# Eight-batch cached attention and dense layers, decode step: a scaled mask for one half of the last batch, and a re-listed order of tasks

## The chip, the cores and the metric

The kernel runs on one core of one Trainium2 chip. The metric is the device time of one execution in microseconds (us). A core has TensorE (PE, with its weight loads shown apart as PEld), VectorE (DVE), ScalarE (ACT), GpSimd (POOL) and SyncE (SP), which here only issues the transfers. The engines run at the same time and wait for each other through semaphores. Lines such as L878 are lines of the kernel before.

## The reference

Eight batches with one query token each (width 448) go through two equal layers. Layer 2 is the same mathematics with the same weights and the same caches.

```python
W = min(4096, max(256, Sk // 4))                       # 1024 keys
q = (x @ wq).reshape(B, Sq, 16, 256)
k, v = the last W rows of k_cache, v_cache, each of 8 heads repeated twice
scores = einsum("bhqd,bhkd->bhqk", q, k) * (256 ** -0.5)
o = einsum("bhqk,bhkd->bhqd", softmax(scores), v) ... @ wo
x = x + A(layernorm(x));  x = x + silu(layernorm(x) @ w1) @ w2     # twice
```

The layer norm divides by the deviation of x. In layer 2 the kernel leaves this division to the end: the query is built from x and its mean only, the scores of all keys are taken with it, and the softmax multiplies them by 1/deviation on the way into the exponential.

## The kernel before, in words

Keys and values of a batch (8 heads, each 512 KB of keys and as much of values) are loaded once and used by both layers. They go through a ring of 30 slots of one head each; every slot is loaded in two halves of 256 KB. SP issues the loads in a fixed order, keys of a batch and then its values. A load waits until its slot has been given back, and until the load ten halves ahead of it has landed. A key slot is given back when layer 2's scores of its four heads are done, a value slot when layer 2's products with the values are. The weights (wq first, wo, w1 and w2 after the first batch) are loaded once.

For each batch, in this order of dependence:

- **KT** (L1238): VectorE turns the 16 key halves in place, 32 x 32 blocks, one instruction each.
- **S0**, layer 1 scores (L878), for all 8 heads; maximum (max0, L889), two small turns and a minimum that bring the maxima of a row together (L896, L898, L901), exponential (L908), transposition of the probabilities on TensorE (pT, L914) and copy (L923), row sums (l, L927) and reciprocal (L932).
- **PV0** (L947), products with the values, in steps for heads 0 to 3 and 4 to 6, and head 7 in another form (L981); `oev` (L952) copies them out, `oT` (L954) transposes; **wor** (L998) multiplies by wo; `fold` (L1014, L1015) brings rows back to columns.
- **chain**: statistics (s12, L1032; m2, mean, va; a reciprocal root by two Newton steps on VectorE), **w1** (L839), its turn (L848), the activation, **w2r** (L998 again), fold, statistics of layer 2 (Newton steps on POOL, L746 to L762, whose result is 1/deviation).
- Layer 2's query, once for heads 0 to 3 and once for 4 to 7: **wq** (L1100, 16 matmuls), turn **qT** (L1105), selection **qsel** (L1111), **qf** (L1117, adds the mean's part, which ScalarE has written at L1091) and **qbd** (L1118), which spreads the query over the four blocks of 32 partitions by multiplying it with a mask of ones and zeros.
- **S1**, layer 2 scores (L878 again), separately for the two halves, the same softmax with 1/deviation as the exponential's scale, and PV1 (L947). Only in the last batch is the softmax itself done for each half apart, as soon as its scores are there. In layer 2 the negated maximum, which is the exponential's bias, is first multiplied by 1/deviation too: **mbs1** (L905).

After batch 7, `final` does layer 2's output product and dense part for all batches at once (L1127 to L1212).

The batches overlap: batch b's layer 2 runs among the steps of batch b+1's layer 1. Each engine executes its instructions in one list, fixed when the program is built. A planner (`schedule`, twice, with priorities from a backward pass `tails`) lists the tasks by estimated costs. It also puts in **fillers** on TensorE (L1282), matmuls that compute nothing and add zero, at places where the planner sees TensorE waiting. Then `best_schedule` goes through the table `MOVES`: an entry `i:j` takes task i out of its engine's list and puts it back directly ahead of task j, one after the other. The task numbers count the tasks in the order in which they are added; the fillers come last, from 1672 on. Those that matter below:

| number | task |
|---|---|
| 217, 245 | s12 of batch 0, first and second |
| 226 to 230, 237 | w1 and w2r of batch 0 |
| 261 to 264, 266 | wq and qsel of batch 0, heads 0 to 3 |
| 265, 267, 268 | qT, qf, qbd of batch 0, heads 0 to 3 |
| 277 to 280 | S1 of batch 0, heads 0 to 3 |
| 346 to 361 | the 16 key turns of batch 1 |
| 362 to 365 | S0 of batch 1 |
| 885 to 888, 869 | PV1 of batch 3, heads 4 to 7, and its row sums |
| 1697, 1704, 1706 to 1715 | fillers |

In the list of before TensorE runs, in batch 0: fold 239, s12 245, wq 261 to 264, x_init of batch 1, fillers 1706, 1708 and 1704, qsel 266. VectorE runs: turns 346 to 349, qT 265, qf 267, turn 352, qbd 268, and then the eleven other turns of batch 1. `rstds[1]` is 1/deviation of layer 2.

Of the kernel before, what the change touches and what calls it, by code (L numbers as in the profile page):

```python
# [51 lines left out]

MOVES = {
# [8 lines left out]
    "dve":  # L62
# [5 lines left out]
    "act":  # L68
# [3 lines left out]
    "pool":  # L72
        "",
}
# [385 lines left out]
def bass_interleave_layers__sliding_block_cached__dense_activation_silu__decode_kernel(  # L460
# [121 lines left out]
    def bk(i):  # L582
        return [("bank", i)]
# [306 lines left out]
            mseg[layer][:, ks[0]:ks[-1] + 1], bank[sc][:, lo:hi].rearrange("p (k n) -> p k n", k=len(ks)), AX.X, ALU.max,  # L890
            negate=True), bk(sc), [("mseg", layer, k) for k in ks], 0.42 if len(ks) == 1 else 0.7, "max%d" % layer)

    def softmax(b, layer, ks, sc):
        lb, ei, mT = LB[layer], layer, mTs[layer]
        row_max(layer, ks, sc)
        dve(lambda e: e.transpose(mT, mseg[ei]), [k for k in MROW[ei] if k[0] != "mT"], [("mT", ei)],  # L896
            0.21, "mT%d" % layer)
        dve(lambda e: e.tensor_reduce(  # L898
            mg[ei][:, 0:4].rearrange("p (k r) -> p k r", r=2),
            mT[:, 0:16].rearrange("p (k q r) -> p k r q", k=2, r=2), AX.X, ALU.min), [("mT", ei)], [("mg", ei)], 0.16, "mg%d" % layer)  # L900
        dve(lambda e: e.transpose(mb[ei].rearrange("p (k q r) -> p k q r", k=4, r=2),  # L901
                                  mg[ei][:].rearrange("p (k r) -> p k r", r=2).unsqueeze(2).broadcast_to([P, 4, 4, 2])),
            [("mg", ei)], [k for k in MROW[ei] if k[0] != "mT"], 0.21, "mb%d" % layer)
        if layer:
            act(lambda e: e.activation(mb[ei][:, 0:2], mb[ei][:, 0:2], ACTF.Copy, scale=rstds[1][:, 0:1]),  # L905
                MSEG[ei] + [("rstd", 1)], MSEG[ei], 0.2, "mbs1")
        for k2 in ks:
            act(lambda e, k2=k2: e.activation(  # L908
                e_sb[ei][:, k2, :, :].rearrange("p uh (jj ul) -> p uh jj ul", ul=2),
                bank[sc][:, k2 * 256:(k2 + 1) * 256].rearrange("p (ul uh jj) -> p uh jj ul", ul=2, uh=4),  # L910
                ACTF.Exp, bias=mb[ei][:, k2:k2 + 1],
                scale=rstds[1][:, 0:1] if layer else 1.0), bk(sc) + [MSEG[ei][k2]] + ([("rstd", 1)] if layer else []), [("e", ei, k2)] + ([] if layer or not k2 else ["rowpad"]), 0.56 if layer else 0.475, "exp%d" % layer)
        for k2 in ks:
            pe([lambda e, uh=uh, ql=ql, k2=k2: e.matmul(  # L914
                bank[lb][64 * ql:64 * ql + 64, k2 * 64:k2 * 64 + 64].rearrange(
                    "p (j q u r) -> p u j q r", j=4, q=2, u=4)[:, uh],
                e_sb[ei][:, k2, uh, :],
                ident[:].rearrange("p (j x) -> p j x", j=4)[:, :, 8 * k2:8 * k2 + 8].rearrange(
                    "p j (qh ql r) -> p j qh ql r", qh=2, ql=2)[:, :, :, ql, :],
                start=True, stop=True, tile_position=(0, 64 * ql)) for uh in range(4) for ql in range(2)],  # L920
               [("e", ei, k2), "ident"] + ([] if layer or not k2 else ["rowpad"]), bk(lb), (16, 2), "pT%d" % layer)
        k0, k1 = ks[0], ks[-1] + 1
        act(lambda e: e.activation(  # L923
            pT_sb[ei][:, k0:k1].rearrange("p k n u r -> p (k n u r)"), bank[lb][:, k0 * 64:k1 * 64], ACTF.Copy),
            bk(lb), [("pT", ei, k) for k in ks], 0.28, "pTev%d" % layer)
        nk = k1 - k0
        pe([lambda e, u=u, qh=qh: e.matmul(  # L927
            bank[lb][:, C_L:C_L + 8 * nk], ones_b,
            pT_sb[ei][:, k0:k1].rearrange("p k (j q) u r -> p k j q u r", q=2)[:, :, :, qh, u, :],
            start=(u == 0 and qh == 0), stop=(u == 3 and qh == 1)) for u in range(4) for qh in range(2)],  # L930
           [("pT", ei, k) for k in ks] + ["ones_b"], bk(lb), (8 * nk, 1), "l%d" % layer)
        dve(lambda e: e.reciprocal(rl_sb[ei][:, 8 * k0:8 * k1], bank[lb][:, C_L:C_L + 8 * nk]), bk(lb),  # L932
            [("rl", ei, k) for k in ks], 0.25, "rl%d" % layer)
# [138 lines left out]
    def chain(b):  # L1072
# [20 lines left out]
        for k2 in range(2):  # L1093
            parts = [(XB, 0, DH), (YB, DH, DH)] if (tail or WQS) and k2 == 0 else [(XB, 0, 2 * DH)]
            for wb, h0, n in parts:
                for c in range(KC):
                    fns = []
                    for j in range(4):
                        off = (c * HD if c < 3 else 3 * HD - k2 * 2048) + (4 * k2 + j) * 512 + h0
                        fns.append(lambda e, j=j, c=c, wb=wb, off=off, h0=h0, n=n, k2=k2: e.matmul(  # L1100
                            bank[wb][32 * j:32 * j + 4, h0:h0 + n], xn[:, part(c, k2), j, :],
                            wq_sb[:, off:off + n], start=(c == 0), stop=(c == KC - 1),
                            tile_position=(0, 32 * j), skip_group_check=True))
                    pe(fns, [("xn", max(0, part(c, k2) - 2))] + WQ_R, bk(wb), (n, 4), "wq")
                dve(lambda e, wb=wb, h0=h0, n=n: e.transpose(  # L1105
                    qT[:, h0:h0 + n].rearrange("p (c a i) -> p c a i", a=2, i=32),
                    bank[wb][:, h0:h0 + n].rearrange("p (c i a) -> p c a i", a=2, i=32)),
                    bk(wb), (QT0 if h0 == 0 else []) + (QT1 if h0 + n > DH else []), 0.18 + n / 950.0, "qT")
            lb = LB[1]
            qs = bank[lb][:, C_Q + 64 * k2:C_Q + 64 * k2 + 64]  # L1110
            pe([lambda e, qs=qs, j=j: e.matmul(  # L1111
                qs[32 * j:32 * j + 32].rearrange("p (k c r) -> p k r c", k=4, c=8), irep,
                qT[:].rearrange("p (r c i) -> p i r c", r=2, i=32)[:, 0:4],
                start=True, stop=True, tile_position=(0, 32 * j)) for j in range(4)], QT0 + QT1 + ["irep"], bk(lb),
               (256, 4), "qsel")
            qf, QF = mrow[1 - k2][:], MROW[1 - k2]
            dve(lambda e, qs=qs, qf=qf: e.tensor_tensor(qf, qs, qf, ALU.add), bk(lb) + QF, QF, 0.25, "qf")  # L1117
            (pool if k2 and not tail else dve)(lambda e, k2=k2, qf=qf: e.tensor_tensor(  # L1118
                qbd[1][:, :, k2, :].rearrange("p n (q r) -> p n q r", r=2),
                qf.rearrange("p (n r) -> p n r", r=2).unsqueeze(2).broadcast_to([P, 32, 4, 2]),  # L1120
                mask.unsqueeze(1).unsqueeze(3).broadcast_to([P, 32, 4, 2]), ALU.mult),
                QF + MASK_R, [("qbd", 1, k2)], 0.55 if k2 and not tail else 0.4, "qbd")

    def rows8(banks, n, w_sb, rhs, reads, name):
        for i0 in range(0, n, 4):
# [132 lines left out]
    def layer2(b):  # L1258
        chain(b)
        last = b == NB - 1  # L1260
        for k2 in range(2):
# [2 lines left out]
            freed.update((b, "k", 4 * k2 + j) for j in range(4))  # L1264
            pump()
            if last:
                softmax(b, 1, (k2,), sc)
        if not last:
            softmax(b, 1, (0, 1), SC[1])
        for k2 in range(2):  # L1270
# [50 lines left out]
```

## Time and profile before

| | |
|---|---|
| median of 3 runs | 242.47 us (242.2 to 242.66) |
| the profiled execution | 243.63 us, its span 241.9 us |
| busy: PE, DVE, ACT, POOL | 188.5, 152.6, 86.7, 26.2 us |
| read from memory | 77.67 MB, mean 321 GB/s over the span |
| shares of the chain that ended last | PE 46%, DMA 18%, DVE 18%, ACT 7%, SP's queue 5% |

The span counts from the first to the last instruction; the device time of the same execution is 1.73 us longer. "Busy" counts an engine's instructions, whether or not anything waits for them. The chain follows the work back from the last instruction: at each step to what released it, or to the instruction before it on its engine. The transfers fill the first 200 us; the last key and value loads are issued at 193.3 and 203.5 us, and from 212 us on nothing but the computation of the last batch is left.

### The profile page before, as it was taken

To read this page: it belongs to the slowest core of one execution; us is meant where nothing else is said; L and a number is where in the kernel's file an instruction comes from. 1 tells how busy PE (TensorE), PEld (TensorE's weight loads), DVE (VectorE), ACT (ScalarE), POOL (GpSimd) and SP (SyncE) were. 2 spreads that over 40 slices of the span, in tenths; PEclk is the share of its full clock that TensorE was granted. 3 is DMA by queue.
4 is the path that set the end of the run, shared out by engine and by line. 5 is a ranking of instruction groups with operands and counts; after the bars stand their busy time and mean duration, and the time that the engine had idled before them with its cause. 6 is when DMAs were issued, how large, how long until landed. Compare 5 with 4: busy or idle time off the path is not lost.

```text
span 241.9 us, 8437 instructions
## 1 busy us (share of the span) xinstructions
PE 188.5 (78%) x3537; PEld 97.5 (40%) x3567; DVE 152.6 (63%) x425; ACT 86.7 (36%) x292; POOL 26.2 (11%) x125
## 2 busy tenths in 40 slices
PE   1052648878969888978897988889878999899884
PEld 1051113322335345534452544355344535446552
DVE  7359420045964995796489559956985896334433
ACT  2004041023034524541644163446426440543431
POOL 6100000002010031003000300210031004003000
PEclk9999999997999999999999999999999999999999
DMA  5999999999999999999999999999999989300000
GB/s 221 377 365 403 407 400 382 391 377 406 402 406 401 342 384 375 395 340 390 323 387 395 387 348 397 378 379 380 395 397 391 385 278 403 139 3 4 3 3 1
DMA packets 40341, 78.22 MB, mean 323 GB/s; under 512 B 4320, under 2 KB 6512, under 8 KB 39792
## 3 DMA queue, kind: packets, MB, share of 16 engines
q1 hardware_dynamic: 40304, 77.69, 86.9%
q8 instruction: 28, 0.46, 0.7%
q14 instruction: 9, 0.07, 0.1%
HBM read 77.67 MB, written 0.01 MB: 321 GB/s over the span
## 4 chain that ended last, share of the span: by engine, by line
PE 46%; DMA 18%; DVE 18%; ACT 7%; SPq 5%; issue 4%; POOL 1%; DVEq 0%; ACTq 0%
DMA ring<-in_A_k_cache_dram 10%; PE bank L947 10%; DVE ring L1238 8%; PE bank L878 7%; DMA w2o<-in_B_w_dram 6%; PE bank L998 6%; PE bank L1100 4%; PE bank L1282 3%; PE bank L1111 3%; ACT qT L908 3%; SPq L679 3%; DMA ring<-in_A_v_cache_dram 3%; DVE mrow L889 2%; PE bank L914 2%; PE bank L954 2%
## 5 line engine op out<-in xcount | busy, mean ns | idle before, releaser
L1238 DVE STREAM_TRANSPOSE ring<-ring 128x512 uint32<-128x512 uint32 x128 | 81.2, 683 | 9.5 <-DMA ring<-in_A_k_cache_dram 9.5
L878 PE MATMUL bank<-ring,qbd 128*16 128x512 bf16 (+2 forms) x768 | 35.9, 324 | 5.1 <-DVE ring L1238 4.1
L947 PE MATMUL bank<-ring,pT_sb 128*4 128x512 bf16 (+1 forms) x512 | 36.5, 378 | 0.1
L1282 PE MATMUL bank<-wq_sb,smalls 128*128 128x512 bf16 x99 | 29.2, 400 | 0.9 <-issue 0.7
L878 PEld LDWEIGHTS bank<-ring,qbd 128*16 128x16 bf16 (+1 forms) x768 | 19.3, 91 | 18.7 <-DVE ring L1238 5.0
L855 ACT ACTIVATE qbd<-q1s 32x128 bf16<-32x128 bf16 x32 | 10.3, 321 | 46.0 <-PE bank L878 45.4
L1100 PE MATMUL bank<-wq_sb,xn 128*4 128x512 bf16 (+1 forms) x272 | 18.3, 384 | 0.6 <-ACT xn L1082 0.3
L889 DVE TENSOR_REDUCE mrow<-bank 128x2 f32<-128x512 f32 (+1 forms) x17 | 10.9, 643 | 11.8 <-PE bank L878 10.1
L1014 ACT ACTIVATE qT<-bank 128x448 bf16<-128x448 f32 x16 | 8.7, 544 | 24.7 <-PE bank L998 24.7
L914 PE MATMUL bank<-ident,qT 128*64 128x16 bf16 x256 | 8.4, 182 | 10.9 <-ACT qT L908 10.5
L1282 PEld LDWEIGHTS bank<-wq_sb,smalls 128*128 128x128 bf16 x129 | 10.8, 100 | 12.5 <-issue 8.2
L947 PEld LDWEIGHTS bank<-ring,pT_sb 128*4 128x4 bf16 (+1 forms) x512 | 11.2, 84 | 10.5 <-issue 1.6
L998 PE MATMUL bank<-w2o,oT 128*1 128x448 bf16 x224 | 13.2, 352 | 0.2 <-DMA w2o<-in_A_wo_dram 0.2
L1105 DVE STREAM_TRANSPOSE qT<-bank 128x512 f32<-128x512 f32 (+1 forms) x17 | 11.3, 665 | 2.7 <-PE bank L1100 2.7
L952 ACT ACTIVATE qT<-bank 128x512 bf16<-128x512 f32 x16 | 9.6, 597 | 9.3 <-PE bank L947 5.9
L914 PEld LDWEIGHTS bank<-ident,qT 128*64 128x64 bf16 x256 | 6.2, 113 | 13.9 <-ACT qT L908 13.0
L952 ACT ACTIVATE qbd<-bank 128x512 bf16<-128x512 f32 (+1 forms) x16 | 9.1, 570 | 4.9 <-PE bank L947 3.0
L746 POOL TENSOR_SCALAR smalls<-smalls 128x1 int32<-128x1 int32 x8 | 1.5, 191 | 85.2 <-ACT smalls L1047 55.9
L1111 PE MATMUL bank<-qT,w2o 128*32 128x64 f32 x128 | 8.4, 353 | 2.4 <-DVE qT L1105 1.6
L1249 POOL MEMSET qT<- 128x64 bf16 x8 | 1.2, 153 | 82.5 <-PE bank L954 75.6
L908 ACT ACTIVATE qT<-bank,mrow 128x256 bf16<-128x256 f32 x16 | 6.8, 471 | 7.6 <-DVE mrow L901 7.4
L1042 DVE SCALAR_TENSOR_TENSOR smalls<-bank,smalls 128x1 f32<-128x1 f32 x8 | 1.2, 149 | 12.9 <-ACT smalls L1040 9.4
(182 smaller groups left out, 255.3 us busy)
## 6 DMA issues: line engine op xcount, KB each, us to landing
ring<-in_A_k_cache_dram SPq DMA_DIRECT2D x128, 256.0 KB, 5.9
ring<-in_A_v_cache_dram SPq DMA_DIRECT2D x128, 256.0 KB, 6.3
w2o<-in_A_wo_dram SPq DMA_DIRECT2D x2, 1792.0 KB, 13.0
wq_sb<-in_A_wq_dram SPq DMA_DIRECT2D x3, 1024.0 KB, 6.9
w2o<-in_B_w_dram SPq DMA_DIRECT2D x1, 1568.0 KB, 14.2
w_sb<-in_B_w_dram SPq DMA_DIRECT2D x3, 448.0 KB, 11.6
wq_sb<-in_A_wq_dram SPq DMA_DIRECT2D x2, 256.0 KB, 10.3
w_sb<-in_B_w_dram SPq DMA_DIRECT2D x2, 112.0 KB, 11.4
```

Of the source, the lines that this page charges most:

```text
L878: fns.append(lambda e, cb=cb, par=par, j=j, kv=kv, m=m, c0=c0, c1=c1: e.matmul(bank[sc][32 * j:32 * j + m, c0:c1], qbd[layer][:, j * 8 + c ...
L889: dve(lambda e: e.tensor_reduce(mseg[layer][:, ks[0]:ks[-1] + 1], bank[sc][:, lo:hi].rearrange("p (k n) -> p k n", k=len(ks)), AX.X, ALU.m ...
L908: act(lambda e, k2=k2: e.activation(e_sb[ei][:, k2, :, :].rearrange("p uh (jj ul) -> p uh jj ul", ul=2), bank[sc][:, k2 * 256:(k2 + 1) * 2 ...
L914: pe([lambda e, uh=uh, ql=ql, k2=k2: e.matmul(bank[lb][64 * ql:64 * ql + 64, k2 * 64:k2 * 64 + 64].rearrange("p (j q u r) -> p u j q r", j ...
L947: fns.append(lambda e, qh=qh, uh=uh, j=j, vv=vv: e.matmul(bank[ob][32 * j:32 * j + 2 * w, 0:w * DH], p_col(ei, k2, j, qh, uh, w), vv, star ...
L952: act(lambda e: e.activation(o_sb[oi][:, 0:w * DH], bank[ob][:, 0:w * DH], ACTF.Copy), bk(ob), O_K[oi], 0.2 + w * 0.2, "oevh" if ob == OB[ ...
L998: pe([lambda e, i=i, c=c: e.matmul(bank[XB][32 * c:32 * c + 1, 0:D], rhs(i), w_sb[:, i * D:(i + 1) * D], start=(first and i - i0 < 4), sto ...
L1100: fns.append(lambda e, j=j, c=c, wb=wb, off=off, h0=h0, n=n, k2=k2: e.matmul(bank[wb][32 * j:32 * j + 4, h0:h0 + n], xn[:, part(c, k2), j, :],
L1105: dve(lambda e, wb=wb, h0=h0, n=n: e.transpose(qT[:, h0:h0 + n].rearrange("p (c a i) -> p c a i", a=2, i=32), bank[wb][:, h0:h0 + n].rearr ...
L1111: pe([lambda e, qs=qs, j=j: e.matmul(qs[32 * j:32 * j + 32].rearrange("p (k c r) -> p k r c", k=4, c=8), irep, qT[:].rearrange("p (r c i) ...
L1238: dve(lambda e, v=v: e.transpose(v, v), [("slot", s, h)], [("slot", s, h)], 0.67, "KT")
L1282: fills = {n: [lambda e, j=j, m=P // n: e.matmul(bank[OB[0]][m * j:m * j + m, 0:2 * DH], zero_b.broadcast_to([P, m]), wq_sb[:, 0:2 * DH], ...
```

## The change

In the last batch, for heads 4 to 7 only, ScalarE multiplies the mask by 1/deviation into four new columns (`masks`), and qbd uses this copy. So the scores of these heads come out scaled. Their softmax is called with `scaled=True`: mbs1 is left out, and the exponential's scale is the constant 1.0. One task is added and one goes away, so the tasks between them have numbers one higher than in before.

```diff
-    def softmax(b, layer, ks, sc):
+    def softmax(b, layer, ks, sc, scaled=False):
         lb, ei, mT = LB[layer], layer, mTs[layer]
+        scale, rk = (rstds[1][:, 0:1], [("rstd", 1)]) if layer and not scaled else (1.0, [])
...
-        if layer:
+        if rk:
             act(lambda e: e.activation(mb[ei][:, 0:2], mb[ei][:, 0:2], ACTF.Copy, scale=rstds[1][:, 0:1]),
...
-                scale=rstds[1][:, 0:1] if layer else 1.0), bk(sc) + ...
+                scale=scale), bk(sc) + ...
...
+            mkey, mk = MASK_R, mask
+            if tail and k2:
+                mkey, mk = ["masks"], smalls[:, 19:23]
+                act(lambda e: e.activation(smalls[:, 19:23], mask, ACTF.Copy, scale=rstds[1]), MASK_R + [("rstd", 1)], ["masks"], 0.2, "masks")
+            mk = mk.unsqueeze(1).unsqueeze(3).broadcast_to([P, 32, 4, 2])
...
-                softmax(b, 1, (k2,), sc)
+                softmax(b, 1, (k2,), sc, k2 == 1)
```

The table `MOVES` is replaced. The planner lists the changed tasks anew, and the table works on that list; 196 tasks stand elsewhere in the order than before. The entries that the prediction speaks of (those that are only in one of the two tables, except 1705:269, 277:272, 1709:1710 and 1714:280, which are in both):

```diff
 "pe"
-"1606:1573 1605:1559 888:869 887:888 1710:279 1704:266 1707:239 1697:1702"
+"1606:1574 1605:1560 888:876 1766:869 887:1766 1715:279 1710:1715 1706:1709 1697:245 1707:1697 1704:237"
 "pe", in both
 "1714:280 1709:1710 277:272 1705:269"
 "dve"
-"361:357 359:358 351:359 352:268"
+"351:360 354:353 350:267"
 "act"
-"1188:1176 1174:1173 1170:1174 1087:928 903:902 618:614 445:434 444:428 371:370 531:530 345:195"
+"1627:1626 1430:1235 1433:1432 1171:1188 1172:1171 1170:1173 1149:1147 986:985 963:961 1088:1087 1089:1088"
...
```

Task 876 is batch 3's first transposition after PV1, 1766 a filler. No entry of the new table names `masks` (1558).

More of the change, by code (lines that the diff above doesn't have):

```diff
@@ L911, in softmax @@
                 ACTF.Exp, bias=mb[ei][:, k2:k2 + 1],
-                scale=rstds[1][:, 0:1] if layer else 1.0), bk(sc) + [MSEG[ei][k2]] + ([("rstd", 1)] if layer else []), [("e", ei, k2)] + ([] if layer or not k2 else ["rowpad"]), 0.56 if layer else 0.475, "exp%d" % layer)
+                scale=scale), bk(sc) + [MSEG[ei][k2]] + rk, [("e", ei, k2)] + ([] if layer or not k2 else ["rowpad"]), 0.56 if layer else 0.475, "exp%d" % layer)
         for k2 in ks:
@@ L1117, in chain @@
             dve(lambda e, qs=qs, qf=qf: e.tensor_tensor(qf, qs, qf, ALU.add), bk(lb) + QF, QF, 0.25, "qf")
[L1118 to L1122, printed above, removed]
+            dst = qbd[1][:, :, k2, :].rearrange("p n (q r) -> p n q r", r=2)
+            qb = qf.rearrange("p (n r) -> p n r", r=2).unsqueeze(2).broadcast_to([P, 32, 4, 2])
+            mkey, mk = MASK_R, mask
[3 more added lines that the diff above has]
+            mk = mk.unsqueeze(1).unsqueeze(3).broadcast_to([P, 32, 4, 2])
+            (pool if k2 and not tail else dve)(lambda e, dst=dst, qb=qb, mk=mk: e.tensor_tensor(dst, qb, mk, ALU.mult),
+                                               QF + mkey, [("qbd", 1, k2)], 0.55 if k2 and not tail else 0.4, "qbd")
     def rows8(banks, n, w_sb, rhs, reads, name):
```

33 rows, old and new, of the table MOVES are left out of this document.

## Prediction, made before the result was known

> **What bounds the kernel now.** The profile of before spans 241.9 us, and the profiled execution took 243.63 us, 1.16 us above the median of the three runs, 242.47. I make the sum as differences inside that execution and take them off the median.
>
> I read the chain of waits first (start, length, what; the piece released the next one), in the stretch where batch 0 hands over to batch 1.
>
> ```profile
> 39.26 14.24 DMA w2o<-in_B_w_dram
> ...
> 56.17 1.81 PE bank L1100 x13
> ...
> 58.14 1.28 PE bank L1282 x3
> 59.42 0.49 PE bank L1111 x8
> ...
> 59.93 0.22 DVE mrow L1117
> 60.16 0.62 DVE ring L1238
> 60.78 0.31 DVE qbd L1118
> 61.08 6.57 DVE ring L1238 x11
> ...
> 67.69 1.04 PE bank L878 x16
> ...
> 147.04 5.26 DMA ring<-in_A_k_cache_dram
> ...
> 228.15 0.54 PE bank L947 x16
> ```
>
> Up to 53.5 us the second weight matrix is landing, so whatever the diff reorders before that is worth nothing. Then comes a piece in which no transfer is late: the 16 query matmuls (L1100), three fillers (L1282), the selection qsel (L1111), and on VectorE qf (L1117), one key turn (L1238), qbd (L1118) and eleven more turns. Only after the last turn can batch 1's scores (L878) start. So three fillers, which compute nothing, are on the path. (The last two lines are used further down.) The table by stretches (length, busy time and count of each engine, clock, DMA share, GB/s) shows why they are so long:
>
> ```profile
> 53.00:56.00 3.00, 1.30 (x23) 0.70 (x24) 1.87 (x3) 1.05 (x6) 0.00 (x0) 0.99 1.05 406
> 56.00:58.00 2.00, 2.00 (x23) 0.56 (x22) 0.71 (x2) 1.08 (x6) 0.83 (x5) 0.50 1.06 407
> 58.00:60.00 2.00, 2.00 (x13) 0.49 (x13) 0.78 (x2) 0.00 (x0) 0.94 (x5) 0.66 1.06 408
> ```
>
> TensorE's granted clock is 0.50 from about 56 us and 0.66 on average in the next 2 us: half clock for 2.0 + 2 x 0.34/0.5 = 3.4 us, right behind a stretch in which TensorE was busy for 1.30 of 3.00 us.
>
> VectorE's timeline there (the bracket is the idle time before, and who ended it):
>
> ```profile
> 54.13 2.58 DVE L1238 STREAM_TRANSPOSE ring<-ring 128x512 uint32<-128x512 uint32 x4 [1.63 <-DMA ring<-in_A_k_cache_dram]
> 58.02 0.72 DVE L1105 STREAM_TRANSPOSE qT<-bank 128x512 f32<-128x512 f32 x1 [1.32 <-PE bank L1100]
> 59.93 0.22 DVE L1117 TENSOR_TENSOR mrow<-bank,mrow 128x64 f32<-128x64 f32 x1 [1.19 <-PE bank L1111]
> ```
>
> VectorE stands still for 1.19 us ahead of qf, because qf is next in its order and qsel is late, while twelve turns wait behind it. From 61 us on those turns are the path.
>
> Whether time won at 67 us reaches the end depends on the loads. Two views speak to that: SP's waits (total, times, longest) and two stretches of the long table.
>
> ```profile
> SPq L710 <- PE bank L947: 15.1, 7, 3.0
> ```
> ```profile
> 50.00:75.00 25.00, 20.41 (x261) 8.14 (x264) 16.42 (x38) 6.57 (x25) 2.39 (x10) 0.93 1.05 402
> 100.00:125.00 25.00, 22.20 (x447) 11.43 (x452) 19.22 (x51) 11.18 (x37) 2.77 (x12) 1.00 1.02 363
> ```
>
> In seven batches the key loads wait, 2.2 us on average, until a layer 2 PV step (L947) has given a slot back, and the loads run at 363 GB/s where 402 has been seen. So the loads follow the computation from batch 2 on, and a shift of it shifts them too.
>
> **The change part by part.**
>
> *The tail, heads 4 to 7.* ScalarE, then TensorE, in before:
>
> ```profile
> 226.91 0.29 ACT L905 ACTIVATE mrow<-mrow,smalls 128x2 f32<-128x2 f32 x1 [0.25 <-DVE mrow L901]
> 227.24 0.56 ACT L908 ACTIVATE qT<-bank,mrow,smalls 128x256 bf16<-128x256 f32 x1
> ```
> ```profile
> 227.04 0.61 PE L947 MATMUL bank<-ring,pT_sb 128*2 128x256 bf16 x16
> 227.86 0.29 PE L914 MATMUL bank<-ident,qT 128*64 128x16 bf16 x8 [0.20 <-ACT qT L908]
> ...
> 229.59 0.61 PE L947 MATMUL bank<-ring,pT_sb 128*2 128x256 bf16 x16
> ```
> ```profile
> L908 ACT ACTIVATE qT<-bank,mrow x16: 467/474/476, 31.7 to 206.2; 128x256 bf16<-128x256 f32 x16
> L908 ACT ACTIVATE qT<-bank,mrow,smalls x16: 555/564/566, 73.5 to 227.2; 128x256 bf16<-128x256 f32 x16
> ```
>
> L905 goes away for these heads: the exponential starts at 226.91 instead of 227.24, 0.33 us. Its scale becomes a constant, so it falls from the second form's 0.564 to the first form's 0.474, 0.09 us. Its result is 0.42 us earlier. TensorE takes less: the 16 PV matmuls ahead of the transpose L914 issue until 227.04 + 0.54 = 227.58 (0.54 is what the chain gives such a step at 228.15), so L914 moves from 227.86 to 227.58: **0.28 us**. From there to 229.59 and the end TensorE has no gap, so all of it is kept.
>
> What is added is one small ScalarE copy with a scale, "masks". The trace has no such 128x4 instruction; the nearest is L905 at 0.29 us, and I bound it by 0.17 (the smallest copies) and 0.29. It needs 1/deviation, POOL's last step:
>
> ```profile
> 222.84 0.19 POOL L762 TENSOR_TENSOR smalls<-smalls 128x1 f32<-128x1 f32 x1
> ```
> ```profile
> 220.23 0.51 ACT L1091 ACTIVATE mrow<-bank,smalls 128x64 f32<-128x64 f32 x2
> 225.15 0.29 ACT L905 ACTIVATE mrow<-mrow,smalls 128x2 f32<-128x2 f32 x1 [4.41 <-DVE mrow L901]
> ```
> ```profile
> 221.45 0.23 DVE L1117 TENSOR_TENSOR mrow<-bank,mrow 128x64 f32<-128x64 f32 x1 [0.65 <-PE bank L1111]
> ...
> 224.13 0.41 DVE L1118 TENSOR_TENSOR qbd<-mrow,smalls 128x256 bf16<-128x256 f32 x1
> ```
>
> It can run from 223.1 to 223.4, inside 4.41 us of idle ScalarE, and qbd, which now waits for it, starts at 224.13. Cover 0.7 us; cost nothing. If that cover went, qbd and all behind it would be late by the rest.
>
> *The moves at batch 0 to 1.* Four of them I can place whatever the planner does, since each is put directly ahead of a named task: key turn 350 goes ahead of qf (267), where before had turn 352 between qf and qbd; filler 1704 ahead of w2r (237), fillers 1707 and 1697 ahead of s12 (245), filler 1706 behind, into batch 0's layer 2 scores. Of the three fillers between the query matmuls and qsel (1706, 1708, 1704) one is left.
>
> ```profile
> 55.88 0.28 PE L1032 MATMUL bank<-xbt 128*128 128x32 bf16 x4 [0.42 <-ACT xbt L1026]
> ...
> 63.42 3.41 PE L1282 MATMUL bank<-wq_sb,smalls 128*128 128x512 bf16 x15
> 67.69 1.04 PE L878 MATMUL bank<-ring,qbd 128*16 128x512 bf16 x16 [0.86 <-DVE ring L1238]
> ...
> 76.20 0.57 PE L981 MATMUL bank<-pT_sb,ring 128*128 128x32 bf16 x16
> ...
> 153.75 1.03 PE L1100 MATMUL bank<-wq_sb,xn 128*4 128x512 bf16 x16
> ```
>
> At half clock a filler takes 1.28/3 = 0.43, at full clock 3.41/15 = 0.23. With one instead of three, TensorE is free at 58.14 + 0.43 = 58.57; qsel's other input, the turn of 58.02, ends at 58.74. So qsel starts at 58.78 instead of 59.42. It took 0.49 with the clock coming back, and may take twice that at half clock; I take 0.75, between the two, and qf starts at 59.55 instead of 59.93. Turn 350 (0.62) fits before it, from 58.74 to 59.36; its keys are the fifth half of that batch, and the four before it came in at 0.65 us each from 54.1, so they are there. Then qf 0.22, qbd 0.31 and eleven turns 6.57: 66.65 instead of 67.65. **1.0 us.** What is late next: the fillers ahead of the scores, which end at 63.42 + 3.41 = 66.83, move 0.64 earlier with qsel and get one more of 0.23: 66.42, not the bound, but close. The values of batch 1:
>
> ```profile
> 57.87 10.02 SPq L716 DMA_DIRECT2D ring<-in_A_v_cache_dram  x16
> ```
> ```profile
> DMA to landing us min/median/max: 3.5/6.3/7.8
> ```
>
> The last is issued at 67.9 and lands at 74.2; head 7's product (L981) ran at 76.20. Up to 2.0 us can be won before values bind. Two fillers (2 x 0.23) ahead of s12 (L1032) fill the 0.42 us in which TensorE waits there.
>
> *The other moves* exchange PV groups with fillers, row sums and w1 steps, or turns with turns. I can't follow them all, since the planner's own order may differ. Bounds: a gain of 0.54 (two PV groups of eight matmuls in the 0.54 step above), a loss of 1.8 (the second rival's). I take 0, because most exchange work that has to be done anyway.
>
> **Sum:** -0.28 - 1.0 = -1.28; 242.47 - 1.28 = **241.2 us**.
>
> **Rivals.** *The half clock goes.* Two fillers put 0.46 us of work into the stretch that was busy for 1.30 of 3.00 us. If that is enough, the query matmuls take the 1.03 of 153.75 and end at about 57.2; the turn (0.72) ends at 57.9, qsel (0.49) at 58.4, key turn 350 at 58.55; then qf, qbd and eleven turns (7.1 in sum) end at 65.7, and 1.9 is won instead of 1.0: 240.3 us. For it: the slow stretch follows the thin one. Against: 1.76 of 3 is still thin. The Trainium skill, "TensorE: Matmul & The Clock Gate", section "What's actually happening", has a free-running 3.4 us window of activity decide between half and full clock; by that rule this rival is what to expect if the threshold is passed. The 3.4 us worked out above agrees with it; no row here shows the threshold.
>
> *Slots come free later; slower.* The diff puts batch 3's last PV group behind the row sum and a filler:
>
> ```profile
> 149.63 0.36 PE L927 MATMUL bank<-pT_sb,smalls 128*128 128x16 bf16 x8
> ```
>
> Its slots then come 0.36 + 0.23 = 0.59 us later, and SP's loads, in order behind it, too. If three batches pay that in full (1.8) and half of the early microsecond is lost with it, the time is 242.47 - 0.28 - 0.5 + 1.8 = 243.5. It decides once SP's wait for L947 grows beyond its 2.2 us a batch. Against: the value slots concerned are read a dozen us later.
>
> *Only the tail counts.* The early microsecond is lost again at a landing, as at 147 us where the chain passes 5.26 us through a key load: 242.2, or 242.47 if the tail's wait is for something else and the change does nothing.
>
> *The mask holds up ScalarE.* If masks stands ahead of L1091 in ScalarE's order, qf waits for POOL: the first of its two copies starts at 223.4 (behind masks) instead of 220.23, so qf at about 223.7 instead of 221.45: 2.2 us, 243.4 with the gains. Against: a planner by readiness puts it into the 4.41 us.
>
> The Trainium skill, same page, section "Architectural detail: the array is 16× 32×32, not 1× 128×128", calls ScalarE's queue strictly first in, first out. By that rule the price is the one above, since nothing behind masks could pass it; no row here shows an instruction of ScalarE passing another.
>
> **How the numbers follow.** Forecast 241.2: 0.40. Clock rival 240.3: 0.22. Tail only 242.2: 0.16. Slots 243.5: 0.19. Mask 243.4: 0.03. A measurement of this kernel tells about 0.2% (0.48 us) from no change; by it faster is 0.62, same 0.16, slower 0.22. The range goes from a little under the clock rival, 240.1, to 242.8, which leaves out most of the two slow cases and little else. The faster cases' own range is 240.1 to 241.9.
>
> **What would show it.** Right: one filler between L1100 and L1111 near 58 us, a turn ahead of qf, batch 1's scores at 66.7 (65.8 with the clock at 1.00), every later batch earlier by as much; in the tail no L905 between the last L901 and L908, L908 at 0.47, and no TensorE idle before L914. Wrong: scores at 66.7 but the last key landing where it was; SP's wait for L947 above 15.1; ScalarE idle shifted ahead of L1091.

## The result and the profile after

The changed kernel takes 241.34 us (median of 22 runs, 240.78 to 243.74), the kernel before 242.44 (22 runs, 241.99 to 244.24). The ratio is 0.9957, with a 95% interval of 0.9938 to 0.9977: 0.43% faster, some 1.1 us. The forecast was 241.2. Here and below the ratio with its interval is estimated from all runs of both kernels; it is not the quotient of the two medians and can differ from it by up to 0.0011.

The two profiles don't show this at first sight. The profiled execution of after took 243.39 us (span 241.6), that of before 243.63: 2.05 and 1.2 us above their medians. So the first thing to find out is what in each of them is not the kernel's.

The handover from batch 0 to batch 1 in after, VectorE's timeline (start, length, engine, line, operation, and in brackets the idle time before it and who ended it):

```profile
57.03 0.72 DVE L1109 STREAM_TRANSPOSE qT<-bank 128x512 f32<-128x512 f32 x1 [0.45 <-PE bank L1104]
57.67 0.67 DVE L1246 STREAM_TRANSPOSE ring<-ring 128x512 uint32<-128x512 uint32 x1
58.39 0.22 DVE L1121 TENSOR_TENSOR mrow<-bank,mrow 128x64 f32<-128x64 f32 x1
58.65 0.44 DVE L1129 TENSOR_TENSOR qbd<-mrow,smalls 128x256 bf16<-128x256 f32 x1
59.01 6.63 DVE L1246 STREAM_TRANSPOSE ring<-ring 128x512 uint32<-128x512 uint32 x11
...
68.22 0.69 DVE L892 TENSOR_REDUCE mrow<-bank 128x2 f32<-128x512 f32 x1 [0.83 <-POOL qbd L1129]
```

The lines have moved down by 3 to 11 (qT is L1109, qf L1121, qbd L1129, a turn L1246, max0 L892). The key turn stands ahead of qf, and the 1.19 us of idle time there is gone. Batch 1's first maximum starts at 68.22; in the profile of before it was 70.23:

```profile
70.23 0.69 DVE L889 TENSOR_REDUCE mrow<-bank 128x2 f32<-128x512 f32 x1 [0.83 <-POOL qbd L1118]
```

That is 2.0 us, twice the 1.0 forecast. The table by stretches (as above: busy time and count of PE, PEld, DVE, ACT, POOL; clock; DMA share; GB/s) says why:

```profile
56.00:58.00 2.00, 1.53 (x27) 0.51 (x26) 1.55 (x3) 0.95 (x6) 0.98 (x5) 1.00 1.06 407
```

The half clock of before isn't there. TensorE next:

```profile
56.95 0.38 PE L1290 MATMUL bank<-wq_sb,smalls 128*128 128x512 bf16 x1
57.80 0.52 PE L1115 MATMUL bank<-qT,w2o 128*32 128x64 f32 x8 [0.47 <-DVE qT L1109]
...
65.70 1.04 PE L881 MATMUL bank<-ring,qbd 128*16 128x512 bf16 x16 [0.54 <-DVE ring L1246]
```

One filler (L1290) is left ahead of qsel (L1115), which now waits for VectorE's turn of the query, and the scores (L881) still wait for the last key turn. Batches 1 to 5 keep the 2.0 to 2.4 us; then they go. In the chain and in TensorE's timeline:

```profile
155.61 6.14 DMA ring<-in_A_v_cache_dram
```
```profile
161.89 1.95 PE L951 MATMUL bank<-ring,pT_sb 128*4 128x512 bf16 x18 [0.63 <-DMA ring<-in_A_v_cache_dram]
```
```profile
156.00:162.00 6.00, 4.55 (x92) 2.42 (x86) 2.68 (x9) 3.61 (x10) 0.61 (x1) 1.00 1.05 402
162.00:164.00 2.00, 2.00 (x26) 0.64 (x19) 0.00 (x0) 0.63 (x2) 0.00 (x0) 0.57 1.05 399
164.00:166.00 2.00, 2.00 (x41) 1.09 (x39) 0.91 (x3) 0.71 (x3) 0.00 (x0) 0.58 1.05 405
...
170.00:172.00 2.00, 2.00 (x38) 0.87 (x37) 1.76 (x9) 0.55 (x3) 0.00 (x0) 1.00 0.74 234
```

Batch 5's PV step (L951) waits for a value, then TensorE runs at 0.57 and 0.58 of its clock for 4 us, and the loads later fall to 234 GB/s; that the slots came back late by it is the likely reason. Batch 6's first maximum is at 182.63, where before had 182.78. So each profile has one stretch of half clock on the path, before at 56 us, after at 162 us. Which of the two belongs to its kernel had to be tried.

The tail of after, ScalarE and the chain:

```profile
222.83 0.30 ACT L1127 ACTIVATE smalls<-smalls 128x4 f32<-128x4 f32 x1 [2.26 <-POOL smalls L765]
...
226.94 0.47 ACT L912 ACTIVATE qT<-bank,mrow 128x256 bf16<-128x256 f32 x1 [0.25 <-DVE mrow L905]
```
```profile
227.14 0.54 PE bank L951 x16
227.68 0.23 PE bank L918 x8
```

masks (L1127) runs in 0.30 us of idle ScalarE; the second half's exponential (L912) has no mbs1 ahead of it and takes 0.47; the transposition L918 stands right behind the PV step. This is what the forecast said.

### The profile page after: what moved, and what is told of

Its sections match the earlier page's. It is cut to its first block, busy times and chain, and to the rows that moved or that the text cites. A ratio compares the mean times of both kernels' runs of the same rounds, so it can differ in the third digit from the quotient of the medians.

```text
span 241.6 us, 8467 instructions
## 1 busy us (share of the span) xinstructions
PE 195.4 (81%) x3567; PEld 96.7 (40%) x3567; DVE 153.2 (63%) x425; ACT 86.6 (36%) x292; POOL 26.3 (11%) x125
## 4 chain that ended last, share of the span: by engine, by line
PE 44%; DMA 27%; DVE 13%; SPq 6%; ACT 6%; issue 3%; POOL 0%; DVEq 0%; ACTq 0%
DMA ring<-in_A_k_cache_dram 16%; DMA ring<-in_A_v_cache_dram 11%; PE bank L951 9%; PE bank L881 6%; PE bank L1002 6%; PE bank L1104 5%; DVE ring L1246 4%; PE bank L1290 3%; SPq L682 3%; PE bank L1115 3%; ACT qT L912 2%; PE bank L842 2%; PE bank L918 1%; DVE mrow L892 1%; PE bank L985 1%
## 5 line engine op out<-in xcount | busy, mean ns | idle before, releaser
L1246 DVE STREAM_TRANSPOSE ring<-ring 128x512 uint32<-128x512 uint32 x128 | 81.1, 682 | 9.3 <-DMA ring<-in_A_k_cache_dram 9.3
L881 PE MATMUL bank<-ring,qbd 128*16 128x512 bf16 (+2 forms) x768 | 36.3, 324 | 4.0 <-DVE ring L1246 3.2
L951 PE MATMUL bank<-ring,pT_sb 128*4 128x512 bf16 (+1 forms) x512 | 38.3, 385 | 0.8 <-DMA ring<-in_A_v_cache_dram 0.6
L1290 PE MATMUL bank<-wq_sb,smalls 128*128 128x512 bf16 x129 | 38.6, 382 | 0.0
L881 PEld LDWEIGHTS bank<-ring,qbd 128*16 128x16 bf16 (+1 forms) x768 | 18.8, 91 | 18.7 <-DVE ring L1246 4.8
L892 DVE TENSOR_REDUCE mrow<-bank 128x2 f32<-128x512 f32 (+1 forms) x17 | 11.1, 650 | 11.7 <-PE bank L881 10.0
L1104 PE MATMUL bank<-wq_sb,xn 128*4 128x512 bf16 (+1 forms) x272 | 17.3, 370 | 0.3 <-ACT xn L1086 0.3
L951 PEld LDWEIGHTS bank<-ring,pT_sb 128*4 128x4 bf16 (+1 forms) x512 | 11.3, 84 | 11.9 <-issue 3.8
L1290 PEld LDWEIGHTS bank<-wq_sb,smalls 128*128 128x128 bf16 x129 | 10.4, 97 | 12.5 <-issue 7.1
L918 PE MATMUL bank<-ident,qT 128*64 128x16 bf16 x256 | 8.5, 183 | 7.5 <-ACT qT L912 7.0
L1109 DVE STREAM_TRANSPOSE qT<-bank 128x512 f32<-128x512 f32 (+1 forms) x17 | 11.3, 665 | 2.2 <-PE bank L1104 2.0
L918 PEld LDWEIGHTS bank<-ident,qT 128*64 128x64 bf16 x256 | 6.3, 116 | 12.6 <-ACT qT L912 11.9
L936 DVE RECIPROCAL mrow<-bank 128x16 f32<-128x16 f32 x8 | 2.1, 258 | 13.4 <-PE bank L931 13.4
L912 ACT ACTIVATE qT<-bank,mrow 128x256 bf16<-128x256 f32 x17 | 7.3, 470 | 8.6 <-DVE mrow L905 8.4
L1115 PE MATMUL bank<-qT,w2o 128*32 128x64 f32 x128 | 8.4, 352 | 2.3 <-DVE qT L1109 1.6
```

The source lines that it names most:

```text
L881: fns.append(lambda e, cb=cb, par=par, j=j, kv=kv, m=m, c0=c0, c1=c1: e.matmul(bank[sc][32 * j:32 * j + m, c0:c1], qbd[layer][:, j * 8 + c ...
L892: dve(lambda e: e.tensor_reduce(mseg[layer][:, ks[0]:ks[-1] + 1], bank[sc][:, lo:hi].rearrange("p (k n) -> p k n", k=len(ks)), AX.X, ALU.m ...
L912: act(lambda e, k2=k2: e.activation(e_sb[ei][:, k2, :, :].rearrange("p uh (jj ul) -> p uh jj ul", ul=2), bank[sc][:, k2 * 256:(k2 + 1) * 2 ...
L918: pe([lambda e, uh=uh, ql=ql, k2=k2: e.matmul(bank[lb][64 * ql:64 * ql + 64, k2 * 64:k2 * 64 + 64].rearrange("p (j q u r) -> p u j q r", j ...
L951: fns.append(lambda e, qh=qh, uh=uh, j=j, vv=vv: e.matmul(bank[ob][32 * j:32 * j + 2 * w, 0:w * DH], p_col(ei, k2, j, qh, uh, w), vv, star ...
L1109: dve(lambda e, wb=wb, h0=h0, n=n: e.transpose(qT[:, h0:h0 + n].rearrange("p (c a i) -> p c a i", a=2, i=32), bank[wb][:, h0:h0 + n].rearr ...
```

## The experiments

**Theory:** the gain is the handover's turn order and the tail, and each is kept to the end; the half clock in both profiles is an accident of the execution. **Rivals:** the half clock in batch 0 is part of the kernel before, and the fillers drive it off; the gain is lost again at batch 5's values; the other moves of the list carry the result.

All times are medians of 10 to 12 runs beside some 30 of before on the same chip; the ratio is to that before. The last two columns are from each kernel's profile: from the start of batch 0's w2r to the start of the first maximum (max0) of batch 1 and of batch 7. In ten of the thirteen profiles the landing of its weights releases w2r (in after_again, after_old_handover and both_gaps VectorE's hT does), so differences in the landing drop out. The profiled executions of this table lie from 0.6 us under (turn_only) to 1.0 us above (tail_only) the median of their kernel, so differences of a few tenths at batch 7 can belong to the execution.

| kernel | time, us | before, us | ratio, 95% | w2r to batch 1 | w2r to batch 7 |
|---|---|---|---|---|---|
| after_again | 241.69 | 242.42 | 0.9959 (0.9934 to 0.9983) | 14.75 | 149.23 |
| tail_only | 242.27 | 242.42 | 0.9987 (0.9967 to 1.0006) | 16.53 | 150.60 |
| order_only | 241.63 | 242.42 | 0.9970 (0.9941 to 1.0000) | 14.75 | 149.11 |
| handover | 241.81 | 242.42 | 0.9965 (0.9943 to 0.9987) | 14.73 | 148.75 |
| before_again | 242.19 (one) | 242.45 | | 15.17 | 149.28 |
| turn_only | 241.98 | 242.45 | 0.9977 (0.9963 to 0.9990) | 14.75 | 148.76 |
| fill_only | 242.45 | 242.45 | 1.0000 (0.9984 to 1.0015) | 15.19 | 149.32 |
| handover_tail | 241.60 | 242.45 | 0.9959 (0.9936 to 0.9983) | 14.75 | 148.75 |
| after_old_handover | 241.97 | 242.66 | 0.9964 (0.9938 to 0.9990) | 15.19 | 150.21 |
| mask_first | 243.10 | 242.66 | 1.0023 (0.9998 to 1.0048) | 14.76 | 148.35 |
| both_gaps | 241.68 | 242.66 | 0.9949 (0.9925 to 0.9974) | 14.60 | 148.99 |

**after_again**: the changed kernel, not edited, for a second profile.

> The changed kernel once more, for a second profile. In its first profile batch 1's scores start 2.0 us earlier than before (65.70 against 67.69), but at batch 6 only 0.13 us are left, lost where a value load of batch 5 landed late. Theory (the handover and the tail make the gain, and it is passed on): in most executions that landing is not late, so this profile keeps 1 us or more of the 2.0 up to batch 6's scores and the time is 241.3. Rival (the gain is always lost at the loads, and the measured gain comes from other moves): the early 2.0 us are gone again at batch 6 here too.

This execution took 241.94 us, with the clock at 1.00 throughout. Batch 1's max0 is at 68.14, and the same stretches behind batch 5's values read:

```profile
156.00:162.00 6.00, 4.36 (x94) 2.63 (x88) 2.68 (x9) 3.72 (x10) 0.61 (x1) 1.00 1.05 402
162.00:164.00 2.00, 2.00 (x48) 0.95 (x40) 0.47 (x3) 0.81 (x2) 0.00 (x0) 1.00 1.05 402
...
170.00:172.00 2.00, 1.36 (x24) 0.61 (x22) 1.90 (x8) 0.91 (x2) 0.00 (x0) 1.00 0.98 353
```

TensorE had the same work ahead of 162 us as in the first profile, yet its clock stayed up, and the loads keep 353 GB/s where they had 234. Batch 6's max0 is at 180.91 instead of 182.63. So the 1.7 us that went with the half clock are that execution's, not the kernel's. Of the 2.0 us against the first profile of before, 1.87 are left at batch 6 (180.91 against 182.78), as the theory wanted; but that profile of before has its own half clock, as the next run shows. What stays is a short wait for a value at the same place:

```profile
161.49 1.25 PE L951 MATMUL bank<-ring,pT_sb 128*4 128x512 bf16 x18 [0.52 <-DMA ring<-in_A_v_cache_dram]
```

**before_again**: the kernel before, not edited, for the same reason.

> The kernel before once more, for a second profile: in the first one TensorE ran at half clock from 56 to 59.4 us, and that execution took 243.63 us, 1.2 us above the median. Theory (the slow stretch belongs to that execution and not to the kernel): here the clock is 1.00 from 53 to 60 us, batch 1's scores start at about 66.4 instead of 67.69, and the time is 242.0 to 242.5. Rival (the slow stretch is always there, as the prediction had it): half clock again, scores at 67.7.

```profile
56.98 0.72 DVE L1105 STREAM_TRANSPOSE qT<-bank 128x512 f32<-128x512 f32 x1 [0.44 <-PE bank L1100]
58.33 0.22 DVE L1117 TENSOR_TENSOR mrow<-bank,mrow 128x64 f32<-128x64 f32 x1 [0.64 <-PE bank L1111]
58.47 0.70 DVE L1238 STREAM_TRANSPOSE ring<-ring 128x512 uint32<-128x512 uint32 x1
59.09 0.38 DVE L1118 TENSOR_TENSOR qbd<-mrow,smalls 128x256 bf16<-128x256 f32 x1
59.40 6.63 DVE L1238 STREAM_TRANSPOSE ring<-ring 128x512 uint32<-128x512 uint32 x11
...
68.61 0.69 DVE L889 TENSOR_REDUCE mrow<-bank 128x2 f32<-128x512 f32 x1 [0.83 <-POOL qbd L1118]
```
```profile
56.00:58.00 2.00, 1.96 (x28) 0.59 (x20) 1.25 (x2) 0.91 (x5) 0.99 (x5) 1.00 1.06 409
```

The same program at full clock: qf starts at 58.33 instead of 59.93 and max0 at 68.61 instead of 70.23. The idle time ahead of qf is 0.64 us, not 1.19. Of the 2.0 us by which the first two profiles differ at batch 1, 1.6 is the clock, so the kernels must be compared with both at full clock. From w2r to max0 (53.44 to 68.61) it is 15.17 us, against 14.75 in after_again: the handover's gain is 0.42 us.

**tail_only**: the code of after with the order of before.

```
-        1606:1573 1605:1559 ... 1563:1558        (before's MOVES)
+        1606:1574 1605:1560 ... 1564:1559        (the same tasks by after's numbers)
```

> The scaled mask alone, every list of tasks as before. Theory: 0.28 us faster, about 242.15, near the edge of what can be told; in the profile no L905 ahead of the last exponential, the exponential at 0.47 us, and TensorE without the 0.20 us of idle time ahead of the last L914. Rival (the wait is taken by something else): no change in the distance from the last qsel to the end.

0.9987 in the timing can't be told from no change, since 0.28 us is 0.12%. This profile has the half clock at 56 us again, which makes its 16.53; the tail isn't touched by that. ScalarE and the chain of tail_only:

```profile
226.83 0.47 ACT L911 ACTIVATE qT<-bank,mrow 128x256 bf16<-128x256 f32 x1 [0.25 <-DVE mrow L904]
```
```profile
227.03 0.54 PE bank L950 x16
227.57 0.22 PE bank L917 x8
...
229.30 0.54 PE bank L950 x16
```

The maximum of the last half (VectorE, before and then tail_only):

```profile
225.75 0.42 DVE L889 TENSOR_REDUCE mrow<-bank 128x1 f32<-128x256 f32 x1 [0.64 <-PE bank L878]
```
```profile
225.67 0.42 DVE L891 TENSOR_REDUCE mrow<-bank 128x1 f32<-128x256 f32 x1 [0.64 <-PE bank L880]
```

The last PV step in the chain of before:

```profile
229.66 0.54 PE bank L947 x16
```

From the maximum to the last PV step it is 229.66 - 225.75 = 3.91 us in before and 229.30 - 225.67 = 3.63 in tail_only: 0.28. It is kept to the end of the span, which comes 16.15 us after that maximum in before, 16.09 in before_again and 15.83 in tail_only.

**order_only** (before's code, after's MOVES by before's numbers) and **handover** (before, with nothing but the lists around qf):

```
 "pe"   - 1710:279 1704:266 1707:239 1697:1702
        + 1715:279 1710:1715 1706:1709 1697:245 1707:1697 1704:237
 "dve"  - 361:357 359:358 351:359 352:268
        + 351:360 354:353 350:267
```

> The new order alone, without the scaled mask. Theory: the handover's gain as in the changed kernel and none of the tail's 0.28: 0.8 us faster than before, about 241.6. Rival (the moves pay only together with the mask): 242.4.

> Before, with only the moves at the handover from batch 0 to batch 1 (one key turn ahead of qf, the fillers 1697, 1704, 1706, 1707, 1715 elsewhere). Theory: batch 1's scores at 65.7 instead of 67.69 with the clock at 1.00, and the time 0.8 to 1.9 us under before, 240.6 to 241.6. Rival (the gain comes from the moves of later batches): batch 1's scores as early, but the time 242.2 or more.

The few entries of handover (0.9965) do what all the moved tasks do (0.9970); the intervals overlap, so a few tenths either way stay possible, and order_only's own interval reaches 1.0000. Both have their gain at the place foreseen, 14.73 and 14.75 us. order_only's median is the 241.6 foreseen; handover's 241.81 misses the 240.6 to 241.6 of its theory by 0.2 us.

**turn_only** and **fill_only** split these entries: the "dve" line alone, and the "pe" line alone.

> Before, with only VectorE's moves at the handover (key turn 350 ahead of qf, and the order of the later turns), all fillers as before. Theory (at full clock the gain of the handover is one key turn of 0.62 us put into VectorE's idle time): 0.6 us faster than before, 241.8, as much as all the moves of the handover together; batch 1's scores at 65.7 to 65.8 with full clock, at 67.0 with half. Rival (the prediction's sum, with 0.38 from the fillers): 0.6 with the fillers' part missing from the 1.0, so handover should be faster than this by 0.4.

> Before, with only TensorE's moves at the handover (one filler instead of three ahead of qsel, two ahead of s12). Theory: at full clock qsel waits for the turn qT and not for the fillers, so 0.0 to 0.15 us; 242.3 to 242.45 and batch 1's scores at about 66.3. Rival (the prediction's): 0.4 us or more, 242.0, and if the fillers take away the slow stretch, 241.5.

The turn brings 0.47 us by the medians (0.9977, 0.56 us by the ratio), the fillers nothing (1.0000). turn_only's VectorE, with all three fillers still ahead of qsel, then fill_only's:

```profile
57.49 0.67 DVE L1240 STREAM_TRANSPOSE ring<-ring 128x512 uint32<-128x512 uint32 x1
58.21 0.23 DVE L1119 TENSOR_TENSOR mrow<-bank,mrow 128x64 f32<-128x64 f32 x1
58.47 0.45 DVE L1120 TENSOR_TENSOR qbd<-mrow,smalls 128x256 bf16<-128x256 f32 x1
58.84 6.63 DVE L1240 STREAM_TRANSPOSE ring<-ring 128x512 uint32<-128x512 uint32 x11
```
```profile
58.58 0.23 DVE L1119 TENSOR_TENSOR mrow<-bank,mrow 128x64 f32<-128x64 f32 x1 [0.64 <-PE bank L1113]
...
59.65 6.63 DVE L1240 STREAM_TRANSPOSE ring<-ring 128x512 uint32<-128x512 uint32 x11
```

From qf to the eleven turns it is 0.63 us in turn_only, 1.07 in fill_only and in before_again: 0.44 us won. It isn't the whole turn of 0.62: with a turn between them, qf's successor started 0.14 us after qf (58.33 to 58.47), without one qbd starts 0.26 after it (58.21 to 58.47), and from qbd to the next turn it is 0.37 instead of 0.31. The stretch from w2r to max0 agrees: 14.75 with the turn moved, 15.19 with the fillers alone. And the gain reaches batch 7: 148.75 or 148.76 in the three kernels that have the moved turn and before's other moves, 149.28 and 149.32 in before_again and fill_only, which have neither that turn nor a half clock at the handover. The reason that the fillers are worth nothing stands in fill_only's PE:

```profile
57.14 0.38 PE L1284 MATMUL bank<-wq_sb,smalls 128*128 128x512 bf16 x1
57.99 0.52 PE L1113 MATMUL bank<-qT,w2o 128*32 128x64 f32 x8 [0.48 <-DVE qT L1107]
```

With two fillers fewer, TensorE waits 0.48 us for the turn of the query. At full clock the three fillers (0.81 us in before_again) end as the turn does.

**handover_tail**: the code of after, before's MOVES with the two lines of handover.

> The scaled mask and the moves at the handover, all other moves as before. Theory (these two places make the whole change): as fast as the changed kernel, 241.3 to 241.6. Rival (the moves of batches 2 to 7 bring part of it): 0.3 us or more slower than the changed kernel, 241.7 or more.

0.9959, as after_again: the handover and the mask are enough for the whole gain, as far as the timing can tell. From w2r to the end of the span its profile takes 186.05 us, against 186.96 in before_again and 186.82 in fill_only: 0.8 to 0.9 us.

**after_old_handover**: after, with the two lines of handover undone.

> The changed kernel with the lists of the handover as before (turn 352 between qf and qbd, the fillers where they were); the scaled mask and all the other moves stay. Theory (turn and mask make the change): only the mask's 0.28 us is left, 242.1 to 242.2. Rival (the moves of the later batches bring something): 241.9 or less.

A miss. With the turn's half microsecond lost it should have come clearly behind after; it came to 0.9964 against before, which can't be told from after's 0.9957. The turn was lost (15.19 us from w2r to batch 1), so the other moves or the scatter make up for it. Its twelve executions fall into two groups, six of 241.21 to 241.65 us and six of 242.29 to 243.16, so the median of 241.97 stands for neither. The profiled one, 242.85, is of the second.

The profiles can't decide between these. Up to batch 7's max0 the kernels with all the moves show 148.35 (mask_first, whose order is after's until then), 149.11 and 149.23 with the new handover and 150.21 without it, all but the load phase at full clock. The profiles that differ do so at a landing. TensorE waits for values of batch 5 in after_again (the 0.52 us above), but not in handover_tail. In after_old_handover it doesn't wait there either; VectorE's turns wait for keys, of batch 4 and of batch 5:

```profile
127.49 1.31 DVE L1247 STREAM_TRANSPOSE ring<-ring 128x512 uint32<-128x512 uint32 x2 [0.83 <-DMA ring<-in_A_k_cache_dram]
...
147.58 0.71 DVE L1247 STREAM_TRANSPOSE ring<-ring 128x512 uint32<-128x512 uint32 x1 [0.89 <-DMA ring<-in_A_k_cache_dram]
```

From batch 1 to batch 5 after_again is 0.69 us quicker than before_again (89.37 against 90.06, max0 at 157.51 and 158.67), and after_old_handover 0.54 slower (90.60). So the other moves can win time up to batch 5, and how much of it is left behind the landings changes from execution to execution; whether the median execution gains or loses by them stays open. What the run does show is that the turn isn't the only way to the gain: with the mask and the other moves half of its executions are as quick as after.

**mask_first**: after, with masks ahead of the two copies L1091 in ScalarE's list.

```
 "act"  + 1558:1536
```

> The changed kernel with the masks instruction put directly ahead of the two copies of L1091 (L1095 in the changed kernel) in ScalarE's list. Theory (ScalarE executes its list in order): the first copy waits until 1/deviation is there and masks is done, about 3 us later than now, and qf and all behind it by 2.2 us, less what then lies beside other work: 243.5 to 243.8. Rival (the copies' wait is covered by the query matmuls and the turn): under 0.5 us lost, 241.9 or less.

ScalarE and VectorE, in that order:

```profile
220.76 0.30 ACT L1128 ACTIVATE smalls<-smalls 128x4 f32<-128x4 f32 x1 [2.56 <-POOL smalls L766]
220.97 0.50 ACT L1096 ACTIVATE mrow<-bank,smalls 128x64 f32<-128x64 f32 x2
```
```profile
218.44 0.45 DVE L1110 STREAM_TRANSPOSE qT<-bank 128x256 f32<-128x256 f32 x1 [0.51 <-PE bank L1105]
221.37 0.23 DVE L1122 TENSOR_TENSOR mrow<-bank,mrow 128x64 f32<-128x64 f32 x1 [2.48 <-ACT mrow L1096]
```

The same qf in after_again:

```profile
220.01 0.23 DVE L1121 TENSOR_TENSOR mrow<-bank,mrow 128x64 f32<-128x64 f32 x1 [0.64 <-PE bank L1115]
```

The rival's mechanism is real: the copies stand behind masks, and qf waits 2.48 us for them. Its price is 2.93 us from the turn of the query to qf, where after_again has 1.10 (218.91 to 220.01): 1.83 us, and in the timing 1.0023 against 0.9957, 1.6 us. The prediction had 2.2, and the 243.10 lies under the 243.5 to 243.8 of this run's theory and far above the rival's 241.9. ScalarE passed no instruction over the waiting one. The Trainium skill, "TensorE: Matmul & The Clock Gate", section "Architectural detail: the array is 16× 32×32, not 1× 128×128", calls its queue strictly first in, first out; this run agrees, with the 1.83 us.

**both_gaps**: after with "352:268" kept too, so that one turn stands ahead of qf and one between qf and qbd, to win the 0.12 us in which qbd waits for qf.

> The changed kernel with one more turn moved: 350 ahead of qf as now, and 352 between qf and qbd as before, so that the 0.26 us between the starts of qf and qbd hold a turn. Theory (at the handover VectorE is the bound): the eleventh turn behind qbd ends 0.15 us earlier against the start of qT; in the time that is too little to tell, 241.2 to 241.5. Rival (qbd's 0.5 us later start holds up batch 0's scores and the fillers behind them, which become the bound): the same or up to 0.3 us slower.

The stretch up to batch 1 is 14.60 us against 14.75, the 0.15 foreseen, but 0.9949 is no clear win over 0.9957. Its TensorE:

```profile
63.09 3.20 PE L1291 MATMUL bank<-wq_sb,smalls 128*128 128x512 bf16 x14
66.33 1.05 PE L882 MATMUL bank<-ring,qbd 128*16 128x512 bf16 x16
```

The scores now start right behind the fillers (63.09 + 3.20 = 66.29) with no wait for a key turn, where after still waited 0.54 us; the last turn ends at the same time (66.28, by VectorE's timeline). So TensorE's own fillers are the next bound at this place, as the prediction's "not the bound, but close" had it. No kernel that ran is clearly faster than after.

## Why the prediction was right, and where only its sum was

- **Handover, the turn ahead of qf:** right mechanism, size 0.44 us in the profile (turn_only, timing 0.47) where 0.62 was put.
- **Handover, two fillers less ahead of qsel, qf 0.38 earlier:** wrong; 0 measured (fill_only). The step took the profile's half clock for the kernel's own. At full clock the fillers hide behind the turn of the query.
- **The clock rival:** the two first profiles seemed to prove it (2.0 us at batch 1), but before_again ran the handover at full clock and took 242.19, near the median of 242.45. One stretch of 3.4 us at half clock takes 1.7 of some 241 us off the mean clock, which makes 0.993, and before and tail_only, whose profiles have the stretch at the handover, show just that. Of the 93 other executions of before beside these runs only 13 have 0.993, with a median of 243.8; the 78 with 1.00, 0.986 or 0.979 have 242.4. So what the rival wanted to win isn't in the median of before. Nor do the fillers drive the stretch off: 2 of fill_only's 12 executions have 0.993 (243.33 and 243.54 us). The "thin" stretch of the prediction, 1.30 of 3.00 us, is thin in part by a missing record: the trace has the weight load of a filler at 54.48 us and no matmul for it, and before_again, the same program, shows 1.83 of 3.00.
- **Tail:** right to the hundredth in the profile: 0.28 by the chain of tail_only, exponential 0.47, the transposition right behind the PV step; the timing of tail_only is too coarse for it. The reason given for its being kept, that TensorE has no gap up to the end, is wrong: behind 232 us TensorE waits four times in before, 2.24 us in all. But these waits are for steps that follow from TensorE's own results, so they move with it. Masks cost nothing: 0.30 us at 222.99 in tail_only, done 0.76 us ahead of qbd at 224.05, where 0.7 of cover was forecast.
- **Only the tail counts:** half of this rival is in after_again, where 0.05 us of the 0.42 is left at batch 7's max0 (149.23 against 149.28), behind a landing as it said. With before's other moves the gain stays, and the timing of after is not that of the tail alone.
- **Other moves, 0:** open. After_again and handover_tail fit it; after_old_handover, as quick without the turn, doesn't.
- **Slots come free later:** not seen. SP's wait for PV steps (now L951) is 12.8 us in all in after_again, 14.0 for L947 in before_again.
- **Fillers close to being the bound, mask on ScalarE:** both mechanisms are there, as both_gaps and mask_first show; neither decided.

The sum by the profiles is 0.44 + 0.28 = 0.72 us, the timing says 1.1 with an interval of 0.56 to 1.5. So the mechanisms of the turn and the mask are right, but that the forecast of 1.28 lay so near the result is luck: a step worth nothing was added to one that was sized too large, and the timing came out above what the two steps explain. That last part, 0.2 to 0.4 us (handover_tail's profile has 0.8 to 0.9), isn't settled; the other moves or the scatter of the timing can hold it.

## What to carry to other kernels

Look at the granted clock around a wait before you price what stands there: a stretch at half clock may belong to the execution and not to the kernel, and a second profile of the unchanged kernel tells. The distance of a profiled execution from the median is the hint: 1.2 and 2.05 us here, where the two stretches cost 1.6 and 1.7. The mean clock of each execution, where it is recorded, tells how common the stretch is. On an engine that runs its list in order, an independent instruction that is ready belongs into the idle time ahead of a waiting one, and filler work belongs where the other input of the next step is late anyway; but count what the moved instruction covered at its old place (here 0.18 of 0.62 us).

## What the runs showed of the hardware

**The slow stretch comes and goes.** The same kernel ran batch 0's handover at 0.50 (before) and at 1.00 (before_again), and after ran batch 5 at 0.57 and at 1.00. In after, two slices of 2 us at 0.57 and 0.58 are 2 x (0.43 + 0.42) / 0.5 = 3.4 us at half clock, as the 3.4 us found before the result. In the 13 profiles the time at half clock, counted like this from the table, is a whole multiple of that: 3.4 us (before, tail_only, after), 6.8 (turn_only), 10.2 (handover, before_again, after_old_handover, mask_first, both_gaps) or none (the other four). Whether the activity just ahead decides can't be read from the busy time: it is 4.55 of 6 us where the clock fell and 4.36 where it didn't, but in the second a filler's matmul is missing from the trace, whose weight load it has at 158.34 us. The Trainium skill, "TensorE: Matmul & The Clock Gate", section "What's actually happening", says that the window of activity is free-running and doesn't start with the kernel; a shift of the window against the kernel would give such differences, and the lengths fit a fixed window, but no run here shows where its edges lie. What the stretch costs depends on where it falls: 1.6 us at the handover; in handover's own profile the table shows 0.60, 0.50 and 0.62 between 32 and 44 us, while the weights were landing, and there it cost that kernel nothing that can be seen: its w2r waited for the landing anyway, and its 14.73 and 148.75 us are those of the others.

```profile
32.00:36.00 4.00, 2.74 (x40) 1.13 (x40) 0.26 (x1) 1.35 (x5) 0.00 (x0) 0.60 1.05 405
36.00:40.00 4.00, 3.05 (x37) 1.44 (x39) 0.51 (x3) 1.09 (x2) 0.16 (x1) 0.50 1.06 385
40.00:44.00 4.00, 4.00 (x12) 1.45 (x11) 0.00 (x0) 0.00 (x0) 0.00 (x0) 0.62 1.06 388
```

**POOL's small steps stretched beside VectorE.** In after_again a step of the Newton chain took longer while VectorE's qbd ran (220.26 to 220.68); in mask_first, where VectorE was idle then, the same step took 0.19. In before_again it was the step ahead of it, 0.37 from 220.37. POOL in after_again:

```profile
220.44 0.30 POOL L758 TENSOR_TENSOR smalls<-smalls 128x1 f32<-128x1 f32 x1
```

So 1/deviation came some 0.1 us later in after_again than in mask_first. Between 30 and 226 us the thirteen traces have 624 such steps (POOL, TENSOR_TENSOR, 128x1). 89 of them took 0.22 to 0.46 us, and every one of these ran beside a qbd of VectorE for 0.16 us or more; 28 met a qbd, all but one for 0.11 us or less, and took 0.19 or 0.20, as did the 507 that ran beside turns, beside qf or beside nothing. So the longer steps go with qbd in every case; why, isn't shown, and no run tried it by itself.
